# Splitting the first activation load in two and dropping one warming matmul at the start of a TensorE-bound kernel

## The chip, the cores and the metric

The kernel runs on one core of a Trainium2 chip. The core has a matrix engine (TensorE, PE in the profile; its weight loads are listed as PEld), a vector engine (DVE), a scalar engine (ACT), GpSimd (POOL) and a sync engine (SP) that mostly issues transfers. The metric is the device time of one execution in microseconds; the number compared is the median over several runs.

## The reference

The kernel computes a gate-weighted mix of two branches over the same input x (2048 x 512):

```python
g = _sigmoid((x * gate_w).sum(-1, keepdims=True))
# branch A: real part of a 2-D DFT, as matmuls
a = einsum("bsd,ed->bse", x, dft_hid_re);  b = einsum("bsd,ed->bse", x, dft_hid_im)
y = einsum("ts,bse->bte", dft_seq_re, a) - einsum("ts,bse->bte", dft_seq_im, b)
# branch B: SwiGLU
h = _silu(x @ w1) * (x @ w3);  out = h @ w2
return g * y + (1 - g) * out
```

Here w1 and w3 are 512 x 1376 and w2 is 1376 x 512; the sequence matrices are 2048 x 2048.

## The kernel before, in words

Every fp32 product is made of three matmuls in the fast fp32r form. An operand is split into a rounded high part (`high`, an ACT copy, line 108) and the remainder (`low`, a DVE subtraction, line 111), and `mm3` (line 119) adds high x high, high x low and low x high. On top of that the products are organised in 2 x 2 blocks with seven instead of eight block products, so sums of blocks have to be formed on DVE as well.

The work has two stretches: first the SwiGLU products with w1 and w3, for eleven chunks of their columns and two groups of x's rows (`gate_up`, lines 338 to 398, which is called 21 times), then eight blocks for the sequence DFT, for w2 and for the hidden DFT (`step`, line 864). Only the very beginning matters for this change. It is written out by hand under a manual schedule, from line 401 on, in the order in which each engine is to work.

SP issues all loads on one queue, in this order:

- `load_w(0, 0, 1)` (line 402): the first quarter of the first weight chunk, 128 KB, tile `ws`
- `load_xo(0, "B11")` (line 403, the transfer is on line 200): the first block of x, 128 x 1024 fp32, 512 KB, tile `xs_B`
- `load_w(0, 1, 4)` (line 409): the other three quarters, 384 KB
- `load_xo` for B21, B12 and B22 (line 411), 512 KB each
- `load_w(1)`, `load_w(2)`, `load_w(3)`, 512 KB each; the next one, `load_w(4)`, waits until the first chunk's buffer is free

While the loads are under way, PE runs `WARM` = 11 bf16 matmuls of 128 x 128 by 128 x 512 on a constant (line 407), whose result is not used. They keep PE busy so that its clock is raised before the real work.

Then come the products of the first row chunk (`half`, line 421; its matmuls are on line 432). Each call is six matmuls: two row halves, three terms. I number them from the first real matmul on:

- matmuls 1 to 6: `half(0, 0, 0, 0, True)` on the first weight quarter and B11. Their order is high x high and weight-low x high for the first half of the block's columns (512 of the 1024), the same for the second half, and last the two terms that need the low part of x. So matmul 1 needs only the high part of the first half of B11.
- matmuls 7 to 12: `half(1, 0, None, 0, True)` on the last weight quarter (`a21`) and B11
- matmuls 13 to 18: `half(0, 0, 1, 1, False)` on the second weight quarter and B21. The order is the three terms of the first half, then of the second; matmul 15 is the first that needs the low part of B21, that of its first half.
- matmuls 19 to 24 and on: the remaining combinations, on B21, B12 and B22

The high part of the first half of B11 and of B21 is made by two engines at once: `split_by_both` (line 446) lets ACT copy 256 columns (line 108) while DVE casts the other 256 (line 449). The low part follows on DVE (line 111); the second half is split in the ordinary way, ACT and then DVE.

Of the kernel before, what the change touches and what calls it, by code (L numbers as in the profile page):

```python
# [21 lines left out]
NG = NST // 2  # L22
NC = (F + P - 1) // P
NP2 = (NC + 1) // 2
WARM = 11
LOOK = 3
K = 9
W2_AT = (9, 11, 13, 15)
# [4 lines left out]
def fnet_swiglu_gate_kernel(  # L33
# [20 lines left out]
    nc = tc.nc  # L54
# [25 lines left out]
    def bank(k, name):  # L80
        return psum.tile([P, 512], F32, tag=f"ps{k}", name=name)
# [14 lines left out]
    def wide(name):  # L96
        return take(F4, [P, 1024], F32, name)
# [91 lines left out]
    XO, ST = {}, {}  # L189
    XRAW = ("B12", "B11", "B21", "B22")  # L190
# [4 lines left out]
    def load_xo(g, k):  # L195

        if g not in XO:
            XO[g] = (xo1 if g else xo0).tile([P, 2, 7, 2, 512], F32R, tag="xo", name=f"xo{g}")
        ST[g, k] = wide(f"xs{g}_{k}")
        nc.sync.dma_start(ST[g, k], xt[g, XRAW.index(k)])  # L200

    OPS = ("B11", "B21", "B22", "T1", "T2", "T3", "T4")
    SUMS = {"T1": ("B12", "B11"), "T2": ("B22", "T1"), "T3": ("B22", "B12"), "T4": ("B21", "T2")}
# [197 lines left out]
    ctx.enter_context(tc.manual_schedule())  # L401
    load_w(0, 0, 1)
    load_xo(0, "B11")
    warm = nc.const_aps.tensor(1.0, [P, 512], mybir.dt.bfloat16)
    wps = bank(7, "wps")
    for n in range(WARM):
        nc.tensor.matmul(wps, warm[:, :P], warm, start=True, stop=True)  # L407
    nc.scalar.activation(act0, warm[:, :24], AF.Silu)
    load_w(0, 1, 4)
    for k in ("B21", "B12", "B22"):  # L410
        load_xo(0, k)
# [111 lines left out]
    for k in ("B11", "B21", "B12", "B22"):  # L523
        do(at_end, 1, load_xo, 1, k)
# [78 lines left out]
    n = NI - 1 - LOOK  # L603
# [348 lines left out]
    for i, (src, sp, p) in enumerate(late):  # L952
        blk, b = 1 + i // 2, i % 2
        n = (17, 24)[b]
# [84 lines left out]
```

## Time and profile before

| | |
|---|---|
| median of 3 runs | 709.09 us (709.05 to 709.46) |
| the profiled execution's own time | 708.95 us |
| span of the profiled execution | 707.2 us |
| PE busy | 702.7 us (99% of the span), 3089 matmuls |
| DVE busy | 605.3 us (86%) |
| ACT busy | 370.1 us (52%) |
| POOL busy | 64.2 us (9%) |
| DMA | 172.54 MB, mean 244 GB/s |

The span runs from the first to the last instruction that the profiler recorded; the run's own time is 1.75 us longer. In the rows, the first two numbers of a timeline line are the start and the duration in us; "x6" is the number of instructions merged into the line; what stands in brackets is the idle time of the engine before it and what ended it. "SPq" lines are the issues of transfers. A matmul's recorded duration includes the pipeline's drain, so matmuls that follow each other overlap in the record; their pace is read from the distance of their starts.

### The profile page before, as it was taken

The page shows a single profiled execution, that of the slowest core. Times are in us where ns is not written, and L with a number is a line of the kernel's source. Part 1 is how long each engine was busy: PE and PEld are TensorE (multiplying, and loading weights), DVE is VectorE, ACT ScalarE, POOL GpSimd, SP SyncE. Part 2 cuts the span into 40 slices and gives each one's busy share as a digit, 9 for nine tenths or more (in the row PEclk, how much of TensorE's full clock was granted, in tenths as well). Part 3 has the DMA queues.
Part 4 walks back from the last instruction along what each step waited for, and adds up shares of the span by engine and source line. Part 5 has one row for each costly group of instructions (what it writes and reads, how often), then busy time and mean ns, then how long its engine had stood idle before and what let it go on. Part 6 is the DMA issues. An engine that isn't in the chain of part 4 may idle for free.

```text
span 707.2 us, 8607 instructions
## 1 busy us (share of the span) xinstructions
PE 702.7 (99%) x3089; PEld 579.2 (82%) x3089; DVE 605.3 (86%) x737; ACT 370.1 (52%) x480; POOL 64.2 (9%) x118
## 2 busy tenths in 40 slices
PE   9999999999999999999999999999999999999997
PEld 6888888888888888888888888888888888888886
DVE  7989978887679999877999689969997896898985
ACT  6666555655446754454554454544555454455452
POOL 0011111211010000000110001100110000000000
PEclk9999999999999999999999999999999999999999
DMA  7665546589997566712595238914999971873932
GB/s 282 239 261 228 214 181 255 184 320 352 419 410 273 212 208 237 277 60 89 181 388 220 90 131 322 335 59 180 389 418 416 355 272 53 301 286 134 320 120 89
DMA packets 45547, 172.54 MB, mean 244 GB/s; under 512 B 5312, under 2 KB 5696, under 8 KB 41664
## 3 DMA queue, kind: packets, MB, share of 16 engines
q1 hardware_dynamic: 32608, 118.63, 45.7%
q0 software_dynamic: 12608, 52.97, 18.9%
q8 instruction: 24, 0.39, 0.2%
q10 hardware_dynamic: 288, 0.39, 0.2%
q14 instruction: 19, 0.16, 0.1%
HBM read 114.82 MB, written 57.16 MB: 243 GB/s over the span
## 4 chain that ended last, share of the span: by engine, by line
PE 99%; DVE 0%; ACT 0%; issue 0%
PE P L119 69%; PE X L119 16%; PE Z L119 8%; PE Y L119 4%; PE C L432 2%; PE wps L407 1%; DVE zc L829 0%; ACT zc L827 0%
## 5 line engine op out<-in xcount | busy, mean ns | idle before, releaser
L119 PE MATMUL P<-zo,a 128*128 128x512 f32 x1344 | 304.8, 389 | 0.0
L119 PEld LDWEIGHTS P<-zo,a 128*128 128x128 f32 x1344 | 252.3, 188 | 52.4
L108 ACT ACTIVATE zo<-B 128x1024 fp32r<-128x1024 f32 (+1 forms) x182 | 189.6, 1045 | 190.6 <-PE P L119 101.2
L111 DVE TENSOR_TENSOR zo<-B,zo 128x1024 fp32r<-128x1024 f32 (+1 forms) x182 | 218.0, 1204 | 48.7 <-ACT zo L108 48.2
L119 PE MATMUL P<-zo,H 128*128 128x512 f32 x468 | 106.2, 389 | 0.0
L119 PEld LDWEIGHTS P<-zo,H 128*128 128x128 f32 x468 | 87.8, 188 | 18.2
L675 DVE TENSOR_TENSOR B<-B,B 128x1024 f32<-128x1024 f32 (+1 forms) x78 | 92.9, 1191 | 0.1
L119 PE MATMUL X<-xo,wb 128*128 128x512 f32 x378 | 92.7, 389 | 0.0
L119 PEld LDWEIGHTS X<-xo,wb 128*128 128x128 f32 x378 | 70.9, 188 | 14.7
L119 PE MATMUL P<-zo,Y 128*128 128x512 f32 x336 | 76.3, 389 | 0.0
L119 PEld LDWEIGHTS P<-zo,Y 128*128 128x128 f32 x336 | 63.1, 188 | 13.1
L327 POOL DMA_DIRECT2D hsp<-h x42 | 23.1, 550 | 127.3 <-DVE h L381 76.1
L119 PE MATMUL X<-xo,wa 128*128 128x512 f32 x126 | 32.0, 389 | 0.0
L119 PE MATMUL Y<-xo,wa 128*128 128x512 f32 x126 | 32.0, 389 | 0.0
L119 PE MATMUL Z<-xo,wb 128*128 128x512 f32 x126 | 32.0, 389 | 0.0
L119 PE MATMUL Z<-xo,wa 128*128 128x512 f32 x126 | 32.0, 389 | 0.0
L678 DVE TENSOR_TENSOR B<-B,B 128x1024 f32<-128x1024 f32 x26 | 31.7, 1220 | 0.0
L904 ACT ACTIVATE zu<-P 128x512 f32<-128x512 f32 x32 | 19.1, 598 | 20.4 <-PE P L119 20.4
L375 DVE TENSOR_TENSOR u<-u,X 128x512 f32<-128x512 f32 x21 | 14.4, 688 | 16.8 <-PE X L119 16.8
L119 PEld LDWEIGHTS Y<-xo,wa 128*128 128x128 f32 x126 | 23.6, 188 | 4.9
L119 PEld LDWEIGHTS X<-xo,wa 128*128 128x128 f32 x126 | 23.6, 188 | 4.9
L119 PEld LDWEIGHTS Z<-xo,wb 128*128 128x128 f32 x126 | 23.6, 188 | 4.9
(137 smaller groups left out, 552.2 us busy)
## 6 DMA issues: line engine op xcount, KB each, us to landing
B<-cc SPq DMA_DIRECT2D x64, 512.0 KB, 6.3
hsp<-h POOLq DMA_DIRECT2D x42, 256.0 KB, 3.6
B<-hsp SPq DMA_DIRECT2D x20, 512.0 KB, 10.5
wbsp<-wb POOLq DMA_DIRECT2D x8, 1024.0 KB, 4.2
wb<-wbsp SPq DMA_DIRECT2D x8, 1024.0 KB, 7.5
B<-zsp SPq DMA_DIRECT2D x16, 512.0 KB, 8.4
H<-w2sp SPq DMA_DIRECT2D x6, 1024.0 KB, 9.2
ws<-w SPq DMA_DIRECT2D x11, 512.0 KB, 5.2
```

Source lines behind the costliest of these rows:

```text
L108: nc.scalar.activation(hi, src, AF.Copy)
L111: nc.vector.tensor_sub(lo, src, hi.bitcast(F32))
L119: nc.tensor.matmul(ps, u, v, start=first and n == 0, stop=last and n == 2, skip_group_check=chain)
L327: nc.gpsimd.dma_start(hsp[g, b + k, j // 2, :, j % 2 * 512 : (j % 2 + 1) * 512], h)
L375: nc.vector.tensor_add(u4, u4, x)
L407: nc.tensor.matmul(wps, warm[:, :P], warm, start=True, stop=True)
L432: nc.tensor.matmul(C[i, j], wp(u, slice(r * P, (r + 1) * P)), xp(r, v), start=start and n == 0, stop=not start and n == 5)
L675: nc.vector.tensor_add(t, t, RAW[blk, b, q][:, :n])
L678: nc.vector.tensor_sub(t, RAW[blk, "B12", q], t)
L904: nc.scalar.activation(U[name][:, r], ps[r], AF.Copy)
```

## The change

The load of the first block of x (B11 of the first of the two groups) is issued as two transfers, columns 0 to 511 and 512 to 1023, 256 KB each, one behind the other on the SP queue. All other loads of x stay whole. The number of warming matmuls goes from 11 to 10. What reads the block is unchanged: the operations on its first half now wait for the first transfer only, those on its second half for the second.

```diff
-WARM = 11
+WARM = 10
...
         ST[g, k] = wide(f"xs{g}_{k}")
-        nc.sync.dma_start(ST[g, k], xt[g, XRAW.index(k)])
+
+        n = 1024 if g or k != "B11" else 512
+        for i in range(0, 1024, n):
+            nc.sync.dma_start(ST[g, k][:, i : i + n], xt[g, XRAW.index(k), :, i : i + n])
```

In the compiled program this is one more transfer on SP and one weight load and one matmul less on PE; the order of all other instructions on every engine is the same. Loads signal their landing on eight semaphores in turn, so every later SP load uses the next one of them.

## The prediction

> **What bounds the kernel now.** I read the page first, then the waits of PE's weight loads over the whole run, then the chain in order of time, and last the first 14 us row by row.
>
> ```profile
> span 707.2 us, 8607 instructions
> PE 702.7 (99%) x3089; PEld 579.2 (82%) x3089; DVE 605.3 (86%) x737; ACT 370.1 (52%) x480; POOL 64.2 (9%) x118
> PE 99%; DVE 0%; ACT 0%; issue 0%
> ```
>
> ```profile
> PEld L407 <- issue: 3.3, 10, 0.7
> PEld C L432 <- ACT xo L108: 0.6, 1, 0.6
> PEld C L432 <- DVE xo L111: 0.2, 1, 0.2
> ```
>
> ```profile
> 0.78 4.85 PE wps L407 x11
> ...
> 216.59 486.89 PE P L119 x2148
> ```
>
> PE is the bound from the first microsecond to the last. The second view holds all the waits of its weight loads in 707 us: after the first real matmuls there is none. So the end moves by just as much as the stream of real matmuls is moved, provided that no wait appears that was hidden so far. The third view gives the pace in the long run: 486.89 / 2148 = 0.227 us a matmul. The whole question lies in the start of this stream.
>
> ```profile
> 4.15 0.15 PEld L407 LDWEIGHTS <-const-bfloat16-1.0 128*128 128x128 bf16 x1 [0.28 <-issue]
> 4.57 0.15 PEld L407 LDWEIGHTS <-const-bfloat16-1.0 128*128 128x128 bf16 x1 [0.28 <-issue]
> 5.29 1.16 PEld L432 LDWEIGHTS C<-xo,wa 128*128 128x128 f32 x5 [0.57 <-ACT xo L108]
> 6.62 0.19 PEld L432 LDWEIGHTS C<-xo,wa 128*128 128x128 f32 x1 [0.17 <-DVE xo L111]
> 8.12 2.68 PEld L432 LDWEIGHTS C<-xo,wa 128*128 128x128 f32 x12
> ```
>
> ```profile
> 4.57 1.06 PE L407 MATMUL wps<-const-bfloat16-1.0 128*128 128x512 bf16 x2
> 5.80 0.62 PE L432 MATMUL C<-xo,wa 128*128 128x512 f32 x2
> 6.71 0.42 PE L432 MATMUL C<-xo,wa 128*128 128x512 f32 x1
> 6.96 0.40 PE L432 MATMUL C<-xo,a 128*128 128x512 f32 x1
> 8.34 2.88 PE L432 MATMUL C<-xo,wa 128*128 128x512 f32 x12
> ```
>
> ```profile
> 2.00:4.00 2.00, 2.00 (x6) 0.73 (x5) 0.40 (x1) 0.66 (x3) 0.00 (x0) 1.00 0.98 294
> 4.00:6.00 2.00, 2.00 (x6) 0.95 (x5) 1.04 (x4) 0.94 (x2) 0.00 (x0) 1.00 1.00 375
> ```
>
> The warming matmuls start 0.42 to 0.43 us apart, nearly twice the later pace, though the granted clock (the 1.00 behind the counts in the stretches) reads full: before its first record the column shows nothing. So they run at half speed. The eleventh starts at about 4.57 + 0.43 = 5.00 and holds the array until 5.43. The first real matmul is ready at 5.29 and queues behind it; the second starts at 5.80. Those 0.37 us from 5.43 lie between the slow pace (0.43) and the fast (0.23), so the clock opens at about 5.7. From 5.80 on the pace is fast: I take matmul 15 at 8.34 + 2 x 0.227 = 8.80.
>
> **The warming matmul.** Without the eleventh, the array is free at 5.00 instead of 5.43. If the clock still opens at 5.7, the time won is spent at half speed: by 5.7 one matmul more of real work is done, which is worth one at full pace, 0.23 us, not 0.43. The late start of matmul 7 (6.96 instead of 6.71 + 0.23 = 6.94), behind a wait for the low part of B11, may add 0.02. The gain that PE could hand on is thus 0.25.
>
> **The split load.** Matmul 1 has to be ready by 5.00.
>
> ```profile
> 4.83 0.94 ACT L108 ACTIVATE xo<-xs_B 128x256 fp32r<-128x256 f32 x2 [1.26 <-DMA xs_B<-xt]
> 7.32 0.94 ACT L108 ACTIVATE xo<-xs_B 128x256 fp32r<-128x256 f32 x2 [0.36 <-DMA xs_B<-xt]
> 8.58 1.06 ACT L108 ACTIVATE b<-xs_B 128x1024 fp32r<-128x1024 f32 x1 [0.32 <-DMA xs_B<-xt]
> ```
>
> ```profile
> 4.83 0.29 DVE L449 CAST xo<-xs_B 128x256 fp32r<-128x256 f32 x1 [0.81 <-DMA xs_B<-xt]
> 5.28 1.29 DVE L111 TENSOR_TENSOR xo<-xs_B,xo 128x512 fp32r<-128x512 f32 x2 [0.15 <-ACT xo L108]
> 7.78 1.29 DVE L111 TENSOR_TENSOR xo<-xs_B,xo 128x512 fp32r<-128x512 f32 x2 [0.15 <-ACT xo L108]
> ```
>
> ```profile
> L111 DVE TENSOR_TENSOR xo<-xs_B,xo x5: 686/693/1226, 5.3 to 11.0; 128x512 fp32r<-128x512 f32 x4, 128x1024 fp32r<-128x1024 f32 x1
> ```
>
> ```profile
> 0.74 0.38 SPq L224 DMA_DIRECT2D ws<-w  x1
> 1.18 0.42 SPq L200 DMA_DIRECT2D xs_B<-xt  x1
> 1.65 0.42 SPq L224 DMA_DIRECT2D ws<-w  x1
> 2.11 1.39 SPq L200 DMA_DIRECT2D xs_B<-xt  x3
> ```
>
> ```profile
> ws<-w SPq DMA_DIRECT2D x1, 128.0 KB, 2.4
> xs_B<-xt SPq DMA_DIRECT2D x1, 512.0 KB, 3.6
> ws<-w SPq DMA_DIRECT2D x1, 384.0 KB, 4.4
> xs_B<-xt SPq DMA_DIRECT2D x1, 512.0 KB, 5.2
> ```
>
> ```profile
> DMA packets 673, 2.46 MB, mean 410 GB/s; under 512 B 72, under 2 KB 72, under 8 KB 673
> q1 hardware_dynamic: 673, 2.46, 101.4%
> ```
>
> ```profile
> DMA packets 391, 0.75 MB, mean 375 GB/s; under 512 B 25, under 2 KB 25, under 8 KB 391
> q1 hardware_dynamic: 391, 0.75, 96.8%
> ```
>
> The last column of the four issue rows is the time from issue to landing, so B11 lands at 1.18 + 3.6 = 4.8, the other weights at 1.65 + 4.4 = 6.05 and B21 at 2.11 + 5.2 = 7.3. The last two fences are DMA views of 8 to 14 us (4 KB packets) and of 684 to 686 us (2 KB packets). At 410 GB/s half a block, 262 KB, takes 0.64 us, so the first half should land at best 0.64 earlier, at 4.16; at worst where the whole landed, at 4.8. The landings before lie 1.25 us apart for 512 KB, the rate of the queue, so I take the good end. Splitting it takes ACT 0.94 - 0.5 = 0.42 (two copies overlap in the row: 4.83 to 5.25, when the weight load starts at 5.29) and 0.05 to reach PE: ready at 4.65, ahead of 5.00. The second half lands at about 4.8 plus what smaller packets cost; its high part is on ACT from there for 0.6 us, to 5.5, and matmul 3, which needs it, is due at 5.8. Its low part on DVE is done about 6.3, and matmul 6 is due about 6.45. Nothing of B11 is late any more.
>
> **What the second transfer costs the others.** SP pays one more issue, 1.65 - 1.18 = 0.47 us, and all loads behind it are issued that much later: B21 at 2.58. Before, B21 waits 5.2 us for its landing, and 128 KB alone landed 2.4 after its issue. Add 384 KB at 410 GB/s, 0.96, and B21 could land at 2.58 + 2.4 + 0.96 = 5.9 if the queue were free. It is not: the DMA share is 0.98 and 1.00 from 2 us to 6. So the slot is hidden in the queue, and only the packets count. In the 4 KB stretch a packet holds an engine for 1.014 x 16 x 6 / 601 = 0.162 us, in the 2 KB stretch for 0.968 x 16 x 2 / 366 = 0.085. Eight 4 KB packets on each engine become sixteen of half the size: 16 x 0.085 - 8 x 0.162 = 0.06 us, and one more completion write. I take 0.08 as the delay of everything behind B11; the bounds are 0 and the whole slot, 0.47. SP's own next wait, for the first weight buffer, comes after these issues and is not reached earlier. The load of chunk 3 has to wait for the semaphore that the first half used, free at 4.2 while its issue comes at about 4.9 (2.11 + 1.39 + 3 x 0.47). POOL's queue is not touched.
>
> **Where the gain meets the next wait.** B21 now matters. Its landing at 7.30 is followed by ACT 7.32 to 7.74, by the first DVE subtraction from 7.78, 0.69 long (the tile's row: 686 to 693 ns), to 8.47, and by 0.05 to PE (the row at 6.62: the subtraction before it ended at 5.28 + 1.29 = 6.57). Matmul 15 could load its weights at 8.52, and start 0.11 later (matmul 6: weights at 6.62, and matmul 7 at 6.96 instead of 6.94, so it ran from about 6.73): 8.63. Before, it starts at 8.80. The room is 0.17, less than the 0.25 that PE could bring, and 0.08 of it goes to the later landing. So 0.17 - 0.08 = 0.09 us survive. Matmul 18, which needs the second subtraction (to 7.78 + 1.29 = 9.07, ready at 9.23, due at 8.80 + 3 x 0.227 = 9.48), has 0.25 and does not cut further. Later stages have more room: B12's copy ends at 9.64, while its first matmul is due at 11.1.
>
> **The sum.** 708.95 - 0.09 = 708.86 us for the profiled execution. Its time stands 0.14 below the median of the runs; against that median the forecast is 709.00 us. 0.2% of it, 1.42 us, is about what a measurement of this kernel can tell from no change; the forecast is far inside.
>
> **A rule against splitting.** Landings 4.8, 6.05 and 7.3 lie one transfer apart, so no fixed price of a transfer shows on a full queue. The Trainium skill, "DMA: Bandwidth & Descriptors", section Bandwidth, says to batch transfers to 1 MiB or more; by its fit of 2.0 us fixed cost a transfer (Anatomy of one DMA, for transfers issued by GpSimd), an estimate for the split is 2.0 us more. The trace does not bear that out here, as the distances show.
>
> **The rivals.**
>
> - The whole gain arrives: B21's landing does not move, and its subtraction is used sooner than I think. 709.09 - 0.25 = 708.84. For it: the room of 0.17 hangs on 0.05 and 0.11 from a single place. Chance 0.12.
> - The slot is not hidden: B21 lands 0.47 later, matmul 15 starts at 8.63 + 0.47 = 9.10 instead of 8.80, and the kernel is 0.30 slower: 709.39. It decides from a delay of 0.17 on. Against it: the full queue. Chance 0.16.
> - The split does not do what it says: the first half lands at 4.8 with the second. PE idles from 5.00 to 5.29, real work starts 0.13 earlier at half speed, worth 0.07: 709.02. Chance 0.06.
> - The clock opens later. If an idle gap between warming and real work restarts the count, the 4.9 us from 0.78 to 5.7 begin anew at about 5.0: open at 9.9, 4.2 later, each us costing 1 - 0.227 / 0.427 = 0.47: 2.0 slower, 711.1. It passes 0.2% from 3.0 us later on. It needs a gap, that is, a first half that lands after 4.5; I expect 4.16. Chance 0.04. The Trainium skill, "TensorE: Matmul & The Clock Gate", Part 1, gives a free-running window of about 3.4 us that has to be busy; one window more would by an estimate cost 1.6 us. By that rule neither count nor kind of the matmuls matters, only that PE is busy, and no row here can show where the window lies.
> - A fixed price per transfer is paid in full: 128 KB took 2.4 us where moving it at 410 GB/s takes 0.3, so 2.1. B21 would land at 9.4, matmul 15 start at 10.73, and the kernel be 1.9 slower: 711.0. This is what the rule on batching amounts to. Chance 0.02.
>
> **How the numbers follow.** The forecast has 0.58. Two in a hundred are left for faster by over 0.2%: no row has 1.42 us to give at the start. Slower by over 0.2% are the last two rivals, 0.06. The rest, 0.92, is within 0.2%. The range runs from the whole gain, 708.84, lowered by 0.2 for scatter between runs (709.05 to 709.46 before), to the hidden slot's 709.39, raised by as much: 708.65 to 709.6. The likeliest case's own range is 708.8 to 709.3.
>
> **What would show it.** Right: first real weight load at about 5.0 or sooner, no DMA wait of ACT beyond 4.2 for the first half, matmul 15 held by the DVE subtraction of B21 and starting about 8.7, later starts 0.05 to 0.15 earlier than before throughout. Wrong: B21's copy starting at 7.5 or later; starts of warming pace (0.43) beyond 6 us; a wait of PE at B12 or later that was not there.

## The result, and the profile after

| | before | after |
|---|---|---|
| median | 709.4 us (709.05 to 709.66, 15 runs) | 710.39 us (710.1 to 712.89, 15 runs) |
| ratio | | 1.002, 95% interval 1.0012 to 1.0028 |
| profiled execution, span | 707.2 us | 708.6 us |
| profiled execution, own time | 708.95 us | 710.34 us |

The changed kernel is slower, by 0.99 us in the medians and by 1.39 us between the two profiled executions. The forecast was 709.00 us, with a range of 708.65 to 709.6; the measured median lies above it. (The median of before at the start of this document is that of three runs, the one here that of 15.) The medians differ less than the traces because the profiled execution of before is one of its fastest, 0.45 us below its median; that of the changed kernel is 0.05 below.

The page of the changed kernel, its busy times and its chain:

```profile
span 708.6 us, 8607 instructions
PE 703.1 (99%) x3088; PEld 578.7 (82%) x3088; DVE 605.4 (85%) x737; ACT 370.0 (52%) x480; POOL 64.0 (9%) x118
PE 98%; DMA 1%; SPq 0%; ACT 0%; DVE 0%; issue 0%
```

A transfer now stands in the chain, the load of x. The waits of PE's weight loads over the whole run show where it acts:

```profile
PEld C L435 <- ACT xo L108: 1.8, 3, 0.8
PEld C L435 <- DVE xo L111: 0.6, 2, 0.4
PEld C L435 <- ACT a L108: 0.3, 1, 0.3
PEld C L435 <- DVE a L111: 0.2, 1, 0.2
```

Rows of the timeline of after, up to 12 us, in order of time (lines 108, 111 and 119 are those of before, the later ones have moved by 3):

```profile
0.78 4.13 PE L410 MATMUL wps<-const-bfloat16-1.0 128*128 128x512 bf16 x10 [0.78 <-PEq L1032]
...
1.17 0.90 SPq L203 DMA_DIRECT2D xs_B<-xt  x2
...
2.59 1.38 SPq L203 DMA_DIRECT2D xs_B<-xt  x3
...
4.34 0.42 ACT L108 ACTIVATE xo<-xs_B 128x256 fp32r<-128x256 f32 x1 [0.77 <-DMA xs_B<-xt]
...
4.81 0.30 PEld L435 LDWEIGHTS C<-xo,wa 128*128 128x128 f32 x2 [0.52 <-ACT xo L108]
...
6.36 0.42 ACT L108 ACTIVATE a<-ws 128x256 fp32r<-128x256 f32 x1 [0.76 <-DMA ws<-w]
...
6.83 1.66 PE L435 MATMUL C<-xo,a 128*128 128x512 f32 x6
...
8.35 0.94 ACT L108 ACTIVATE xo<-xs_B 128x256 fp32r<-128x256 f32 x2 [1.04 <-DMA xs_B<-xt]
8.79 1.29 DVE L111 TENSOR_TENSOR xo<-xs_B,xo 128x512 fp32r<-128x512 f32 x2 [0.15 <-ACT xo L108]
8.81 0.30 PEld L435 LDWEIGHTS C<-xo,wa 128*128 128x128 f32 x2 [0.75 <-ACT xo L108]
8.81 3.29 PE L435 MATMUL C<-xo,wa 128*128 128x512 f32 x12 [0.32 <-ACT xo L108]
9.54 2.13 PEld L435 LDWEIGHTS C<-xo,wa 128*128 128x128 f32 x10 [0.43 <-DVE xo L111]
```

Two rows of before for comparison:

```profile
6.02 0.42 ACT L108 ACTIVATE a<-ws 128x256 fp32r<-128x256 f32 x1 [0.26 <-DMA ws<-w]
...
6.96 1.54 PE L432 MATMUL C<-xo,a 128*128 128x512 f32 x6
```

The aim of the split was met: the first half is on ACT at 4.34 (the whole block was at 4.83) and the first real weights load at 4.81 instead of 5.29. PE is 0.49 ahead at matmul 1. That lead is gone before B21 matters: the other three weight quarters, behind the split in the queue, reach ACT at 6.36 instead of 6.02, matmul 7 starts only 0.13 earlier than before, and the six matmuls from there end at 6.83 + 1.66 = 8.49, where they ended before (6.96 + 1.54 = 8.50). Then B21 reaches ACT at 8.35 instead of 7.32, and matmul 13 starts at 8.81 instead of 8.34. PE is 0.47 behind there, and 0.87 behind after the wait for DVE at matmul 15 (the last row of after). From then on nothing changes any more. The long last piece of PE in the two chains, before and then after:

```profile
216.59 486.89 PE P L119 x2148
```

```profile
217.46 486.89 PE P L119 x2148
```

So 0.87 of the 1.39 us is made in the first 10 us, all of it by B21's load. The other half microsecond comes behind the last matmul, a part of the run that the text ahead of the prediction takes as untouched. PE's chain ends at 703.48 before and at 704.35 after, the spans at 707.18 and 708.56: 3.70 us, then 4.21. (From the start of the last matmul it is 4.10 and 4.61; the experiments use this measure.) SP's waits behind 703 us, before and then after:

```profile
SPq L1035 <- DMA out<-zc: 1.1, 3, 0.4
```

```profile
SPq L1038 <- DMA out<-zc: 1.6, 1, 1.6
```

At the end of the program SP waits for the eight completion semaphores one after the other. Before, the store that lands last has the last of the eight: SP has gone through the others by then, in three waits. With one transfer more, the last store has the first of the eight. SP sits at it for 1.6 us, and the other seven, long complete, are read only then, one each 0.06 us: 0.44 in all. The remaining 0.07 is the last store itself, which lands 1.97 us after its issue instead of 1.90.

Why B21 is late is seen in the rate of the transfers. The stretches of 3 to 7 us, before and then after; the last two columns are the DMA share and GB/s:

```profile
3.00:4.00 1.00, 1.00 (x4) 0.31 (x3) 0.40 (x1) 0.42 (x1) 0.00 (x0) 1.00 1.01 393
4.00:5.00 1.00, 1.00 (x4) 0.29 (x2) 0.19 (x2) 0.17 (x1) 0.00 (x0) 1.00 1.02 363
5.00:6.00 1.00, 1.00 (x4) 0.65 (x3) 0.84 (x3) 0.76 (x2) 0.00 (x0) 1.00 0.98 387
6.00:7.00 1.00, 1.00 (x6) 0.71 (x6) 0.91 (x3) 0.94 (x2) 0.00 (x0) 1.00 1.06 422
```

```profile
3.00:4.00 1.00, 1.00 (x4) 0.31 (x3) 0.40 (x1) 0.42 (x1) 0.00 (x0) 1.00 1.12 341
4.00:5.00 1.00, 1.00 (x4) 0.34 (x3) 0.53 (x3) 0.45 (x2) 0.00 (x0) 1.00 0.92 256
5.00:6.00 1.00, 0.89 (x4) 0.41 (x4) 0.85 (x2) 0.60 (x1) 0.00 (x0) 1.00 0.76 239
6.00:7.00 1.00, 1.00 (x5) 0.53 (x4) 0.51 (x2) 0.64 (x2) 0.00 (x0) 1.00 0.83 320
```

In these four microseconds 1565 - 1156 = 409 KB less are moved; at 410 GB/s that is 1.0 us, as much as B21 is late. From 4 us on the DMA engines are idle for up to a quarter of the time, though B21 has been issued since 2.6 us. The queue did run dry, and the prediction had it full.

### The profile page after: what moved, and what is told of

Read it like the earlier page. It is cut to its first block, busy times and chain, and to the rows that moved or that the text cites. A ratio compares the mean times of both kernels' runs of the same rounds, so it can differ in the third digit from the quotient of the medians.

```text
span 708.6 us, 8607 instructions
## 1 busy us (share of the span) xinstructions
PE 703.1 (99%) x3088; PEld 578.7 (82%) x3088; DVE 605.4 (85%) x737; ACT 370.0 (52%) x480; POOL 64.0 (9%) x118
## 4 chain that ended last, share of the span: by engine, by line
PE 98%; DMA 1%; SPq 0%; ACT 0%; DVE 0%; issue 0%
PE P L119 69%; PE X L119 16%; PE Z L119 8%; PE Y L119 4%; PE C L435 1%; DMA xs_B<-xt 1%; SPq L203 0%; SPq L227 0%; DVE zc L832 0%; ACT xo L108 0%; ACT zc L830 0%
## 5 line engine op out<-in xcount | busy, mean ns | idle before, releaser
L119 PEld LDWEIGHTS Z<-xo,wa 128*128 128x128 f32 x126 | 23.7, 188 | 4.9
```

The costliest lines, as they stand in the source:

```text
L119: nc.tensor.matmul(ps, u, v, start=first and n == 0, stop=last and n == 2, skip_group_check=chain)
```

## The experiments

My theory after the result: the extra transfer costs everything, by B21's landing and by the last semaphore; the warming matmul costs nothing. The rivals: the missing warming matmul costs; the small 2 KB rows of the halves are slow; the longer end is scatter of the stores.

**One part at a time.** Only the warming matmul (`WARM = 10`, whole load):

> The load stays whole, only the eleventh warming matmul is left out. Theory (the extra transfer costs everything): B11 and B21 land as before (4.8 and 7.3 us), matmul 15 is not before 8.63, the time is within 0.25 us of before, 0 to 0.2 faster. Rival (the missing warming matmul costs, by a later clock or a gap): 0.5 to 1.4 us slower than before, with slow-paced real matmuls in the trace.

Only the split (`WARM = 11`):

> The load is split, all eleven warming matmuls stay. Theory (the extra transfer costs everything): B21 lands about 1.0 us later than before, at 8.3, matmul 13 starts at 8.8, the end of the program takes 0.5 longer after the last matmul, and the time is that of the changed kernel, 710.4, 1.0 to 1.4 us slower than before. Rival (the missing warming matmul costs): the time of before, 709.1 to 709.6.

Measured: 709.38 us with ten warming matmuls, against 709.19 for the kernel before on the same chip (ratio 1.0005, 0.9996 to 1.0014); the split alone 710.38 (ratio 1.0017, 1.0009 to 1.0026), the time of the whole change. B21 on ACT, first with ten warming matmuls and a whole load, then with the split alone:

```profile
7.47 0.94 ACT L108 ACTIVATE xo<-xs_B 128x256 fp32r<-128x256 f32 x2 [0.36 <-DMA xs_B<-xt]
```

```profile
8.29 0.94 ACT L108 ACTIVATE xo<-xs_B 128x256 fp32r<-128x256 f32 x2 [0.71 <-DMA xs_B<-xt]
```

The split is the whole loss. The warming matmul alone brought nothing that can be measured; in its trace B11 came to ACT at 5.21 instead of 4.83, so PE had a gap of 0.48 us where the time should have been won:

```profile
5.68 1.83 PE L432 MATMUL C<-xo,wa 128*128 128x512 f32 x6 [0.48 <-ACT xo L108]
```

The missing matmul did not make B11 late. In the traces of pad32 and pad64 (below), with eleven of them and the same order of loads, it came at 5.19 and 5.21, and in that of copy1 at 4.90. When the whole B11 lands thus differs between executions, and the trace of before, on which the prediction rests, has the earliest of these. This accounts for the medians too. The profiled execution with ten warming matmuls took 709.37 us, the median of before. Against it the changed kernel starts its last matmul 0.48 us later (703.95 instead of 703.47) and takes 0.51 longer from there: 0.99, the difference of the medians. That the ordinary run of before looks like this one is likely, but not shown: one trace of before was kept.

**Rows or transfers.** The kernel before, whole B11, with an extra load of 64 KB right behind it:

```diff
     load_xo(0, "B11")
+    pad = wup.tile([P, 4, 256], F32, tag="wu", name="pad")
+    nc.sync.dma_start(pad.rearrange("p a n -> p (a n)")[:16], xn[0, :16])  # extra16
+    nc.sync.dma_start(pad[:, 0, :128], xn[0, :, :128])                     # extra128, in its place
```

> The kernel before (whole B11, eleven warming matmuls) with one more SP load of 64 KB, as 16 rows of 4 KB, right behind B11's: one issue slot and hardly any data (64 KB, 0.16 us at 410 GB/s). Theory A (a transfer has a price of its own in supplying its descriptors, whatever it moves): B21 lands 0.5 to 1.0 us later than 7.3 beyond the 0.16, and the time is 0.5 to 1.4 us slower than before. Theory B (the 2 KB packets of the halves are what is slow): B21 at 7.3 to 7.6, 0.4 to 0.6 slower than before, all of it from the last semaphore's place.

> The same with the 64 KB as 128 rows of 512 bytes. If the price goes by rows (descriptors), this one is later than the load of 16 rows, B21 at 8.0 or later, while the one of 16 rows is at 7.5; if it goes by the issue slot, both have B21 at the same time within 0.15 us.

Measured: 710.53 and 710.37 us against 709.36 (ratios 1.0018, 1.0009 to 1.0028, and 1.0018, 1.0008 to 1.0027). B21 on ACT in the two:

```profile
8.30 0.94 ACT L108 ACTIVATE xo<-xs_B 128x256 fp32r<-128x256 f32 x2 [0.51 <-DMA xs_B<-xt]
```

```profile
8.28 0.94 ACT L108 ACTIVATE xo<-xs_B 128x256 fp32r<-128x256 f32 x2 [0.83 <-DMA xs_B<-xt]
```

Without any half, and with 64 KB more data only (0.16 us), B21 is as late as in the changed kernel, and the number of rows does not matter. Theory B of these runs, the small rows, falls: they are not needed for the loss.

**Which queue, and how many.** The same extra load from ACT's queue instead of SP's, and two extra loads of 32 KB on SP. Both have small copies later on that put the last semaphore back:

> Whole B11, eleven warming matmuls; the extra load of 16 rows of 4 KB is issued from ACT's queue at the start, and seven small copies put the last semaphore back. Theory A (a transfer more ahead of B21 on SP's own queue is the price): B21 lands at 7.3 to 7.6, time within 0.3 us of before. Theory B (any transfer more on the 16 engines is the price): B21 at 8.2, 0.5 to 0.9 slower than before.

> The 64 KB as two SP loads of 16 rows of 2 KB each behind B11's, with six small copies that put the last semaphore back. If every transfer ahead of B21 has the same price, about 0.8 to 1.0 us, B21 lands at 9.1 to 9.3, matmul 13 starts at 9.6 to 9.8 and the time is 1.4 to 1.9 above before; if the price is a single one that comes with the fifth transfer of a queue, B21 lands at 8.2 to 8.4 as with one extra load, and the time is 0.5 to 0.9 above before.

Measured: 709.39 us against 709.38 from ACT's queue (ratio 1.0002, 0.9993 to 1.0012), and 709.98 for two more on SP's (ratio 1.001, 1.0001 to 1.002). B21 on ACT:

```profile
7.54 0.94 ACT L108 ACTIVATE xo<-xs_B 128x256 fp32r<-128x256 f32 x2 [0.35 <-DMA xs_B<-xt]
```

```profile
8.46 0.94 ACT L108 ACTIVATE xo<-xs_B 128x256 fp32r<-128x256 f32 x2 [0.97 <-DMA xs_B<-xt]
```

A transfer more costs B21 next to nothing when another queue issues it. (The first weights paid for it: they landed at 4.1 instead of 3.1, in time all the same.) On SP's queue the first one costs 1.0 us and the second 0.16: not a price for each, as I had it under theory A.

**Halves without the extra place.** The first half on ACT's queue, with and without a correction of the last semaphore:

```diff
-            nc.sync.dma_start(ST[g, k][:, i : i + n], ...)
+            (nc.scalar if n == 512 and i == 0 else nc.sync).dma_start(ST[g, k][:, i : i + n], ...)
```

> The changed kernel, but the first half of B11 is issued from ACT's queue, at about 0.74 us, so that SP has as many issues ahead of B21 as before. Theory (SP's chain of issues is what delays B21): B21 at 7.3 or sooner, no wait of PE for it beyond 0.1 us; the end is still 0.5 longer by the semaphores; time 709.3 to 709.9. Rival (the 2 KB packets or a transfer more in all cost it): B21 at 8 or later, time about 710.4.

> The same with seven small loads in the middle of the run, which put the last store's semaphore back. Theory: B21 at 7.3 or sooner and the end as before: 0 to 0.4 us faster than before. Rival (2 KB packets or one transfer more): 0.5 to 0.9 us slower than before.

Measured: B21 landed at 7.7, so the halves themselves do not hold it up for long. But the first weights landed at 4.5 instead of 3.1, PE stood idle from 5.2 to 5.72, and the time was 709.99 us (ratio 1.0016, 1.0005 to 1.0027): 709.8 to 710.0 in five runs, 711.4 to 711.8 in four. The profile caught one of the latter. The pace of its real matmuls:

```profile
5.72 2.90 PE L435 MATMUL C<-xo,wa 128*128 128x512 f32 x6 [0.52 <-DVE xo L452]
8.42 2.01 PE L435 MATMUL C<-xo,a 128*128 128x512 f32 x6
10.26 1.09 PE L435 MATMUL C<-xo,wa 128*128 128x512 f32 x4
```

Six matmuls from 5.72 to 8.42 are 0.45 each, the slow pace; the next six take 1.84, which is 0.48 more than at 0.227, so the clock opened at about 9.4. The throttle record in the packed traces begins where the pace rises: at 9.40 here, at 5.69 in the trace of before. This is the rival "the clock opens later" of the prediction, after a gap of half a microsecond. The Trainium skill, "TensorE: Matmul & The Clock Gate", Part 1, gives a free-running window of 3.4 us that must be busy; by that an opening at 9.4 closes a window that began at 6.0, the first one without the gap, and the trace agrees. How much of a window has to be busy no run here shows: in copy1 the clock opened at 3.55, only 2.8 us after PE's first matmul (0.78). Nor does every gap cost: PE stood still for 0.48 us with ten warming matmuls alone and for 0.93 in extra16_act, and there the real matmuls ran at the fast pace from the start, the clock having opened at 5.32 and 3.90. The version with small loads is told with the next group.

**The end.** One small transfer in the middle of the run, or seven on top of the split, to move the last semaphore. First into a new tile on the chip:

```diff
+    pad = const.tile([P, 8], F32, tag="pad", name="pad")
...
     for n in range(1, NI):
         gate_up(n)
+        if 4 <= n < 5:   # < 11 for seven
+            nc.sync.dma_start(pad[n * 16 - 64 : n * 16 - 48], xn[0, :16, :8])
```

> The kernel before, with one load of 16 rows of 32 bytes into an unused tile in the middle of the run, so that the later loads and stores use the next completion semaphore. Theory (the order in which SP reads the eight semaphores at the end costs): start as before, 4.6 instead of 4.1 us from the start of the last matmul to the end of the span, 0.4 to 0.5 us slower than before. Rival (the longer end of the changed kernel was scatter of the last stores): 4.1 us, within 0.15 us of before.

> The changed kernel with seven such small loads in the middle, so that with the second half eight transfers are added and the last store has the semaphore that it had before. Theory: B21 at 8.3 as in the changed kernel, 4.1 us from the start of the last matmul to the end, 0.5 us faster than the changed kernel: about 709.9, 0.5 to 0.9 slower than before. Rival (scatter): as the changed kernel, 710.4.

The end came out as expected, 4.54 and 4.18 us, but the times were 721.09 and 721.47 us (and 720.9 for the first half on ACT's queue with seven loads): all matmuls had become slower, which says nothing on what the end costs in time. The next ones were made so that no tile moves (a copy from HBM to HBM):

```diff
+    pad = dram.tile([8, 16, 8], F32, tag="pad", name="pad")
...
+            nc.sync.dma_start(pad[n - 4], xn[0, :16, :8])
```

> The kernel before with one small copy on SP's queue in the middle of the run, 16 rows of 32 bytes from HBM to HBM, so that no tile on the chip moves and all later transfers use the next completion semaphore. Theory: pace 0.227 us a matmul as before; 4.5 to 4.6 instead of 4.1 us from the start of the last matmul to the end of the span; 0.4 to 0.5 us slower than before. Rival (the longer end is scatter): within 0.15 us of before.

> The changed kernel with seven such copies, which put the last store's semaphore back. Theory: B21 lands at 8.2 to 8.4 as in the changed kernel, the end takes 4.1 us, and the time is 0.4 to 0.5 below the changed kernel's 710.4, so 0.5 to 0.9 above before. Rival (scatter): 710.4.

> Split load, eleven warming matmuls, seven small copies that put the last semaphore back. If the two costs (B21's later landing and the end) simply add up, this is 0.4 to 0.5 below the split with eleven warming matmuls alone (710.38): 709.8 to 710.0, B21 at 8.2 to 8.4, the end 4.1 to 4.2 us. If the copies cost what they take away at the end, it stays at 710.3 to 710.5.

Measured: one copy in the kernel before gives 709.84 against 709.38 us (ratio 1.0007, 0.9997 to 1.0016), an end of 4.54 us, and SP's wait as in the changed kernel:

```profile
SPq L1038 <- DMA out<-zc: 1.6, 1, 1.6
```

The split with seven copies has the short end, 4.17 us with ten warming matmuls and 4.18 with eleven. Here is SP's wait in the latter, with the three pieces of before:

```profile
SPq L1041 <- DMA out<-zc: 1.2, 3, 0.5
```

Its profiled execution took 709.88 us, 0.41 less than that of the split alone (710.29), the whole of it at the end. But the medians did not come down: 710.43 and 710.7 us. Three runs of ten with ten warming matmuls and four of ten with eleven are at 709.7 to 710.0, as expected; the others lie at 710.2 to 711.2. The trace with ten is one of the upper ones (710.16): B21 is on ACT at 8.59 there, and the last matmul starts 0.27 later than in the changed kernel. No trace shows one of the upper ones with eleven, so where those lose it is open. That the place of the last semaphore makes the end longer is shown by the traces of both directions; that putting it back pays in the median is not.

**The tile's place.** An unused tile of 32 or 64 bytes a partition in the kernel before, which GpSimd fills with zeros once, and no transfer:

> The kernel before with an unused tile of 32 bytes a partition and a memset of it on GpSimd, and no transfer added. If the place of the tiles sets the pace of the matmuls, 0.230 us each and about 721 us, as with the small loads into such a tile; if the small loads did it, 0.227 and the time of before.

> The same with 64 bytes a partition. If the pace depends on the tiles' place in steps of 64 bytes, 0.227 us a matmul and the time of before within 0.5 us; if on any displacement, 0.230 and about 721 us.

Measured, one run each: 720.87 and 717.84 us. The last piece of PE's chain with 32 bytes and with 64, against 486.89 above:

```profile
220.58 494.82 PE P L119 x2148
```

```profile
218.73 493.64 PE P L119 x2148
```

That is 0.2304 and 0.2298 us a matmul instead of 0.2267. PE's weight loads have no wait there after the start, so each matmul is slower by itself. The small loads did not do it; what the versions with the slow pace have in common is the added tile, which moves all tiles allocated after it. Which of the moved tiles slows the matmuls, and why, is not shown.

**What decides in the queue.** Three more, to find the rule behind B21's landing. The first weight chunk in one transfer ahead of the halves; the same with a whole B11; and the extra load behind B21 (small copies keep the last semaphore in its place in the last two):

```diff
-    load_w(0, 0, 1)
+    load_w(0)
...
-    load_w(0, 1, 4)
```

> The changed kernel, but the first weight chunk is loaded in one transfer of 512 KB ahead of the halves of B11, instead of 128 and 384 KB around them: again three transfers ahead of B21 on SP, with the halves among them, and as many transfers in all as before. Theory (one transfer more ahead of B21 on SP's queue is the price, not the halves): B21 lands at 7.0 to 7.5, the end takes 4.1 us, no later than before, at best 0.3 us faster (weights at about 3.7, the first half at about 4.4, first matmul at about 4.9). Rival (transfers of 2 KB rows hold the queue up wherever they are): B21 at 8 or later, 0.5 to 0.9 slower than before.

> The kernel before (whole B11, eleven warming matmuls) with the first weight chunk in one transfer of 512 KB: two transfers ahead of B21 instead of three, the same bytes; one small copy in the middle keeps the last semaphore. If each transfer fewer gains as much as one more cost, B21 lands at 6.3 to 6.6; if only a fourth transfer ahead of B21 costs, it lands at 7.2 to 7.4, set by the bytes. B11 lands at about 5.0 either way and the time is within 0.3 us of before.

> The extra load of 16 rows of 4 KB behind B21 instead of ahead of it, with seven small copies. If a transfer more is paid by what stands behind it, B21 lands at 7.3 to 7.4 and B12 1.0 us late, at 9.4 to 9.6 instead of 8.55; PE then waits for B12 at matmul 25, 11.06 before, by at most 0.6 us. If the full queue hides it by then (B12 has 0.47 us more to be supplied than it needs), B12 lands at 8.6 to 8.8 and the time is that of before within 0.2 us.

Measured: with the whole chunk and the halves 711.86 us (ratio 1.0032, 1.0022 to 1.0041), with the whole chunk and whole B11 709.56 (ratio 1.0003, 0.9994 to 1.0012), with the extra load behind B21 709.72 (ratio 1.0005, 0.9996 to 1.0014), each against 709.31. B21's issue to landing, issued at 2.11 in the first and at 1.65 in the second, and B21 on ACT in the third:

```profile
xs_B<-xt SPq DMA_DIRECT2D x1, 512.0 KB, 5.9
```

```profile
xs_B<-xt SPq DMA_DIRECT2D x1, 512.0 KB, 5.1
```

```profile
8.10 0.94 ACT L108 ACTIVATE xo<-xs_B 128x256 fp32r<-128x256 f32 x2 [0.91 <-DMA xs_B<-xt]
```

The 711.86 us are not a matter of B21. The first half of B11, behind 512 KB of weights, kept PE waiting for 1.44 us, and the granted clock then fell to half from 8.1 to 11.5 us; matmul 13 started at 11.17, long after B21. Its first real matmuls, and one of the stretches at half clock (the 0.50 behind the counts):

```profile
6.45 2.37 PE L434 MATMUL C<-xo,wa 128*128 128x512 f32 x6 [1.44 <-ACT xo L108]
```

```profile
9.00:10.00 1.00, 1.00 (x4) 0.77 (x3) 1.00 (x2) 0.70 (x1) 0.00 (x0) 0.50 1.01 414
```

B21 lands at 8.0, 6.7 and 8.1. The first has three transfers ahead of B21, as the kernel before has, where it lands at 7.3: the count ahead of it does not decide alone, and my theory of these runs falls. In the third, B21 is late although the extra load is issued after it: it isn't only the slot ahead either. What all the versions with a late B21 have in common is one transfer more among the first few on SP's queue than in the kernel to compare each with (for the first of these three, that is the second), and a lower rate while B21 is on its way: between 4 and 7 us in most of them, only from 7 to 8 us in the last (274 GB/s, where copy1 has 414). What in the queue does this, the runs do not tell; the second extra load that costs hardly anything, and the late one that costs almost as much, speak against a simple price per transfer and against a simple order.

No version here beats the kernel before.

## Why the prediction was wrong

- **"So the slot is hidden in the queue, and only the packets count."** This is the step that failed. I read a DMA share of 0.98 and 1.00 in the kernel before as room for 0.47 us of delay. With one transfer more the share fell to 0.76, and B21 landed 1.0 us later, not 0.08, and beyond the upper bound of 0.47 that I had set. The same 0.08 was to hold for the other weights; they came 0.34 later, and PE's lead was lost on them. A full queue before says what it moved, not how much later it could have been fed.
- **The bound of 5.9 us for B21** was worked out from a single transfer on an empty queue (2.4 us). B21 took 5.7 us from its issue, as it had taken 5.2 before, so its time hung on what else was queued. The bound was of no use.
- **The rival "the slot is not hidden"** had the right place (B21, matmul 15) and the right sign. Its price of 0.30 was the slot alone, 0.47 less the room of 0.17; the trace shows 0.87. The rival of a fixed price had 2.1 us for a transfer, twice what was measured, and extra16x2 speaks against a price for each.
- **The end** is missing in the prediction. The text before it notes that every later load uses the next semaphore, and no term was made of it: 0.51 us, 0.44 of them by the order in which SP reads the semaphores.
- **The rule against splitting** was set aside because landings one transfer apart showed no fixed price. The Trainium skill, "DMA: Bandwidth & Descriptors", section Bandwidth, says to batch transfers; in direction the trace agrees with it (1.0 us for one more, on SP's queue), while on ACT's queue the same load cost 0.2 at most.
- **One execution taken for all.** The clock "opens at about 5.7" and the whole B11 lands at 4.8 in the one trace of before. Over the traces here the clock opened at 3.55 to 6.62 us (9.40 in split_act), and the whole B11 of an unchanged queue came between 4.8 and 5.2. In the trace of the changed kernel the clock opened at 4.47, so the real work had full pace from the start: that part of the 0.49 us of lead is luck.
- **Slips in the sums:** 0.94 - 0.5 is 0.44 (the row's times do give the 0.42), and 5.43 - 5.29 is 0.14, not 0.13. Nothing hangs on them.
- **Right:** the first half early (4.34, I had 4.16 to 4.8), real work that starts 0.49 earlier, and matmul 15 held by the subtraction of B21. PE's gain at the start was there, but was used up at matmul 12, before B21. The pace later is the same to the last digit.

## What to carry to other kernels

Splitting a transfer to get its first half early moves all that is queued behind it, so price the next load that the critical engine will need, not only the one that is split, and bound its delay by more than the added issue. At the start of a program a DMA share near 1 is no proof of slack: one transfer more took it to three quarters. And look at the end of the program whenever the number of transfers changes: if semaphores are taken in turn, the last store's place among them may cost half a microsecond.

## What was not expected of the hardware

- An added 64 KB load cost B21 1.0 us on SP's queue and 0.2 on ACT's.
- An unused tile of 32 bytes a partition, which moves the tiles allocated after it, slowed every matmul from 0.2267 to 0.2304 us, 1.6% of the whole kernel, with no wait in between. 64 bytes did nearly the same (0.2298). Each is a single run, and three versions with a tile of 32 bytes and small loads bear the first out (720.9 to 721.5 us).
- The clock did not open at a fixed time: at 5.69 us in the trace of before, 4.47 in that of the changed kernel, 3.55 to 6.62 in all but one. In split_act, with an idle gap of half a microsecond ahead of the real work, it opened at 9.40 in the profiled execution, and some runs of that kernel took 1.5 us more than others. Up to its first opening the granted clock in the profile's rows reads 1.00; only the pace shows it.
- In whole_w_split, after PE had been idle for 1.44 us, the granted clock fell to half for 3.4 us, and this time the rows show it.
